# A block-DFT convolution with decimated rows, issued behind the FFN of the preceding chunk

## The chip, the cores and the metric

The program runs on one core of a Trainium2 chip. The metric is the device time in microseconds. Before the change the median of three runs is 472.5 us (472.4 to 473.94).

## The reference

Two layers, each made of a long convolution (H3 style) and a SwiGLU FFN, both added to the residual x. The sequence has 2048 rows of 512 channels, the FFN is 1792 wide. Inputs are bf16.

```python
k_shift = sum(k_pad[:, t:t + S, :] * shift_k[:, ks - 1 - t] for t in range(ks))   # ks = 4
kv = k_shift * v
y = irfft(rfft(pad(kv)) * rfft(pad(ssm_k)))[:S].astype(bf16) + kv * ssm_D          # along the sequence
A = lambda q: q * y
B = lambda x: (silu(x @ w_gate) * (x @ w_up)) @ w_down
x = A_q
for _ in range(2):
    x = x + A(layernorm(x))
    x = x + B(layernorm(x))
```

The convolution y depends on k, v, shift_k, ssm_k and ssm_D alone. It is the same in both layers and is needed row by row: the first 512 rows of x need the first 512 rows of y.

## The kernel before

The work has two stages, one after the other. **Convolution.** The sequence is cut into four blocks of 512 rows. For each block k and h (ssm_k) are loaded with a transposing DMA and v with a plain one (lines 115 to 129). `kv_block` multiplies 128-row pieces of k with 16 diagonal matrices of taps (256 matmuls of 128x128 in all, line 158) and VectorE multiplies by v (line 160). `forward` takes the odd-frequency DFT of a block, zero-padded to 1024 points, by 32 matmuls of 128x512 (line 171); ScalarE evacuates it to H or X (line 173). The tables are computed on the chip by `_gen_dft_table` (lines 23 to 49): VectorE makes the phase, ScalarE the sine and cosine. `product(i, j)` multiplies the spectra of block i of kv with block j of h and adds the result to Y of block i+j: six or eight VectorE operations of 128x2048 bf16 (lines 196 to 203), ten such pairs. `inverse(k)` turns Y of block k and, for the overlap, Y of block k-1 back into 512 rows: 64 matmuls of 128x512, 32 for block 0 (line 216).

**FFN.** Then, for each layer and each of four chunks of 512 rows: LayerNorm statistics (lines 288 to 298; the power runs on POOL), the convolution's residual in two f32 VectorE operations per 128 rows (lines 313, 315), statistics again, z on ScalarE (324), four transposes on TensorE (328), evacuation to zT (329), 14 steps of gate and up projections (335, 338) with sg on ScalarE (341) and hT_f on VectorE (342), and four down projections of 14 matmuls each (346), whose sum is added to x_sb in f32 (349) or stored (352, 353).

A scheduler orders the instructions of each engine by program order and its own costs. Pools set what may overlap: the weights (lines 231 to 245) take the place of the signal tiles, and the pools of the FFN that of the spectra, so no FFN instruction comes before the convolution's end.

Of the kernel before, what the change touches and what calls it, by code (L numbers as in the profile page):

```python
# [18 lines left out]
CONV_BLOCKS = 4  # L19
ROW_CHUNK = 512  # L20


def _gen_dft_table(nc, tabp, scr, L, kind, pidx):
    N = 2 * L
    KT = L // P
    FD = L if kind == "fwd" else N
    fr = scr.tile([P, FD], F32, name="fr")
    if kind == "fwd":
        nc.gpsimd.iota(fr[:], pattern=[[2, FD]], base=1, channel_multiplier=0, allow_small_or_imprecise_dtypes=True)
    else:  # L30
        nc.gpsimd.iota(fr[:], pattern=[[1, FD]], base=0, channel_multiplier=0, allow_small_or_imprecise_dtypes=True)
    cos_t = tabp.tile([P, KT, FD], BF16, name=f"{kind}_cos")
    nsin_t = tabp.tile([P, KT, FD], BF16, name=f"{kind}_nsin")
    for kt in range(KT):
        mult = scr.tile([P, 1], F32, name="mult")
        if kind == "fwd":
            nc.vector.tensor_scalar(out=mult[:], in0=pidx[:], scalar1=float(kt * P), scalar2=None, op0=ALU.add)
        else:
            nc.vector.tensor_scalar(out=mult[:], in0=pidx[:], scalar1=2.0, scalar2=float(2 * kt * P + 1),
                                    op0=ALU.mult, op1=ALU.add)  # L40
        prod = scr.tile([P, FD], I32, name="prod")
        nc.vector.tensor_scalar(out=prod[:], in0=fr[:], scalar1=mult[:], scalar2=float(N), op0=ALU.mult, op1=ALU.add)
        ms = scr.tile([P, FD], I32, name="ms")
        nc.vector.tensor_single_scalar(out=ms[:], in_=prod[:], scalar=2 * N - 1, op=ALU.bitwise_and)
        nc.scalar.activation(out=nsin_t[:, kt, :], in_=ms[:], func=ACT.Sin, scale=-math.pi / N, bias=math.pi)
        am = scr.tile([P, FD], F32, name="am")
        nc.scalar.activation(out=am[:], in_=ms[:], func=ACT.Abs, scale=1.0, bias=float(-N))
        nc.scalar.activation(out=cos_t[:, kt, :], in_=am[:], func=ACT.Sin, scale=-math.pi / N, bias=math.pi / 2)
    return cos_t, nsin_t
# [3 lines left out]
def kernel(  # L53
# [44 lines left out]
    ypool = tc.alloc_tile_pool(name="ypool", bufs=1, side="left")
    Y_sb = ypool.tile([P, NS, D], BF16, name="Y_sb")
    tabp = tc.alloc_tile_pool(name="tab", bufs=1, side="left")  # L100
    specp = tc.alloc_tile_pool(name="spec", bufs=1, side="left")
    ykp = tc.alloc_tile_pool(name="yk", bufs=4, side="left")
    tmpp = tc.alloc_tile_pool(name="ptmp", bufs=2, side="left")
    psc = tc.alloc_tile_pool(name="psc", bufs=2, space=PSUM)
    tscr = tc.alloc_tile_pool(name="tscr", bufs=1, side="right")
# [281 lines left out]
```

## Time and profile before

| what | value |
|---|---|
| median of three runs | 472.5 us (472.4 to 473.94) |
| span of the profiled execution | 472.5 us, 5517 instructions |
| TensorE matmul busy | 430.5 us, 91% |
| VectorE busy | 289.9 us, 61% |
| ScalarE busy | 167.1 us, 35% |
| chain that ended last | TensorE 70%, VectorE 15%, ScalarE 8% |

The profiled execution's own time is its span, 472.5 us, which is also the median. Busy shares are averages over the whole span. The convolution ends at 128.7 us, the first gate matmul starts at 146.8 us, and the last matmul ends at 468.6 us.

### The profile page before, as it was taken

What the parts mean: (1) busy time and instruction counts of PE and PEld (TensorE: products, weight loads), DVE (VectorE), ACT (ScalarE), POOL (GpSimd) and SP (SyncE); (2) the same over time, 40 slices, a digit from 0 to 9 for tenths busy, and PEclk for the clock granted to TensorE, in tenths of its full rate; (3) what the DMA queues carried; (4) which work ended last, traced back from release to release, by engine and by line L of the source; (5) the groups of instructions that cost most, each with busy time, mean ns of one, the idle gap of its engine ahead of it and who ended that gap; (6) DMA issues with size and microseconds to landing.
All of it is one profiled execution on the core that took longest, in us unless ns stands there. A gap on an engine that the chain in (4) does not pass through costs nothing.

```text
span 472.5 us, 5517 instructions
## 1 busy us (share of the span) xinstructions
PE 430.5 (91%) x2166; PEld 204.8 (43%) x2208; DVE 289.9 (61%) x473; ACT 167.1 (35%) x250; POOL 27.4 (6%) x43
## 2 busy tenths in 40 slices
PE   4999999999927997999999899999989999997996
PEld 3545545544403443444444444444434444443442
DVE  2649899999778899955763774684213423321431
ACT  4995444310115421631432353053153305303320
POOL 7000000000101201100000000000000000000000
PEclk9999999999976999899999999999989999998999
DMA  8925000670211000000000000000000000000001
GB/s 177 183 44 136 2 1 1 222 246 0 90 44 44 1 1 0 0 1 1 1 0 2 0 1 0 1 1 0 16 30 0 1 33 12 1 24 22 0 1 44
DMA packets 26779, 16.39 MB, mean 35 GB/s; under 512 B 17793, under 2 KB 25730, under 8 KB 26754
## 3 DMA queue, kind: packets, MB, share of 16 engines
q1 hardware_dynamic: 26754, 16.05, 12.4%
q8 instruction: 17, 0.28, 0.2%
q14 instruction: 8, 0.07, 0.0%
HBM read 9.70 MB, written 2.10 MB: 25 GB/s over the span
## 4 chain that ended last, share of the span: by engine, by line
PE 70%; DVE 15%; ACT 8%; issue 2%; POOL 1%; SPq 1%; DMA 1%; POOLq 0%; DVEq 0%; ACTq 0%
PE pd L346 19%; PE pu L338 18%; PE pg L335 18%; PE pi L216 10%; PE pf L171 5%; DVE bnst L292 3%; ACT zT L329 3%; DVE x_sb L315 2%; DVE hT_f L342 2%; ACT z L324 2%; POOL rstd L297 1%; DVE t L196 1%; DVE t L197 1%; ACT X L173 1%; ACT H L173 1%
## 5 line engine op out<-in xcount | busy, mean ns | idle before, releaser
L342 DVE TENSOR_TENSOR hT_f<-sg,pu 128x512 bf16<-128x512 bf16 x112 | 76.3, 684 | 90.2 <-PE pu L338 88.2
L335 PE MATMUL pg<-zT,wg_sb 128*128 128x512 bf16 x438 | 116.9, 387 | 4.2 <-ACT zT L329 3.4
L338 PE MATMUL pu<-zT,wu_sb 128*128 128x512 bf16 x439 | 116.8, 386 | 1.7 <-DVE hT_f L342 1.2
L341 ACT ACTIVATE sg<-pg 128x512 bf16<-128x512 f32 x112 | 66.8, 596 | 117.4 <-PE pg L335 110.6
L346 PE MATMUL pd<-wd_sb,hT_f 128*128 128x512 bf16 x438 | 97.8, 379 | 1.7 <-DVE x_sb L349 1.0
L335 PEld LDWEIGHTS <-wg_sb 128*128 128x128 bf16 x448 | 44.6, 99 | 57.8 <-issue 8.6
L338 PEld LDWEIGHTS <-wu_sb 128*128 128x128 bf16 x448 | 44.6, 100 | 56.9 <-issue 6.2
L346 PEld LDWEIGHTS <-hT_f 128*128 128x128 bf16 x448 | 43.8, 98 | 54.4 <-issue 1.3
L329 ACT COPY zT<-pt 128x512 bf16<-128x512 bf16 x32 | 17.8, 584 | 90.5 <-PE pt L328 90.4
L297 POOL TENSOR_TENSOR rstd<-ve,nhalf 128x4 f32<-128x4 f32 x16 | 18.0, 1128 | 288.7 <-DVE ve L295 261.2
L352 DVE TENSOR_TENSOR ot<-x_sb,pd 128x512 bf16<-128x512 f32 x16 | 11.0, 687 | 37.1 <-PE pd L346 37.1
L292 DVE BATCH_NORM_STATS2 bnst<-x_sb 128x6 f32<-128x512 f32 x48 | 31.7, 675 | 0.4
L328 PE MATMUL pt<-ident,z 128*128 128x128 bf16 x128 | 12.3, 232 | 20.6 <-ACT z L324 16.8
L324 ACT ACTIVATE z<-x_sb,nmr,rstd 128x512 bf16<-128x512 f32 x32 | 24.7, 807 | 8.9 <-DVE nmr L319 8.9
L158 PE MATMUL pk<-dg,kTb 128*128 128x128 bf16 x256 | 19.9, 232 | 8.6 <-DMA kTb<-in_A_k_dram 6.5
L216 PE MATMUL pi<-Yk,inv_nsin 128*128 128x512 bf16 x110 | 27.3, 379 | 0.2
L216 PE MATMUL pi<-Yk,inv_cos 128*128 128x512 bf16 x107 | 27.0, 379 | 0.1
L196 DVE TENSOR_TENSOR t<-X,H 128x2048 bf16<-128x2048 bf16 x20 | 24.3, 1215 | 3.4 <-ACT X L173 3.4
L173 ACT ACTIVATE X<-pf 128x1024 bf16<-128x1024 f32 x16 | 16.5, 1030 | 22.3 <-PE pf L171 22.2
L197 DVE TENSOR_TENSOR t<-X,H 128x2048 bf16<-128x2048 bf16 x20 | 24.3, 1215 | 0.0
L158 PEld LDWEIGHTS <-kTb 128*128 128x128 bf16 x256 | 17.4, 105 | 13.3 <-DMA kTb<-in_A_k_dram 6.5
L228 ACT CAST Y_sb<-pi 128x512 bf16<-128x512 f32 x16 | 9.4, 586 | 36.2 <-PE pi L216 30.7
(47 smaller groups left out, 312.4 us busy)
## 6 DMA issues: line engine op xcount, KB each, us to landing
vt<-in_A_v_dram SPq DMA_DIRECT2D x4, 512.0 KB, 4.3
xin<-in_A_q_dram SPq DMA_DIRECT2D x4, 512.0 KB, 3.6
out_dram<-ot SPq DMA_DIRECT2D x16, 128.0 KB, 1.7
wg_sb<-in_B_w_gate_dram SPq DMA_DIRECT2D x1, 1792.0 KB, 7.2
wu_sb<-in_B_w_up_dram SPq DMA_DIRECT2D x1, 1792.0 KB, 11.3
wd_sb<-in_B_w_down_dram SPq DMA_DIRECT2D x1, 1792.0 KB, 16.0
kTb<-in_A_k_dram SPq DMA_TRANSPOSE x4, 5.3
hTb<-in_A_ssm_k_dram SPq DMA_TRANSPOSE x4, 4.3
```

Of the source, the lines that this page charges most:

```text
L158: nc.tensor.matmul(ps[:, dt * P:(dt + 1) * P], lhsT=kTb[:, dt, c0 - j:c0 - j + P], rhs=dg[:, dt, j, :], start=(j == 0), stop=(j == KS - 1))
L196: nc.vector.tensor_mul(out=t1[:], in0=Xi[:, :, pa[0], :], in1=Hj[:, :, pa[1], :])
L197: nc.vector.tensor_mul(out=t2[:], in0=Xi[:, :, pb[0], :], in1=Hj[:, :, pb[1], :])
L216: nc.tensor.matmul(pss[m][:], lhsT=tab[:, ft, c0:c0 + P], rhs=Ysrc[:, ft, part, :], start=(cnt[m] == 0), stop=(cnt[m] == nmm - 1))
L292: nc.vector.bn_stats(out=st[:], in_=src_of_tile(i))
L324: nc.scalar.activation(out=z[:], in_=x_sb[:, n0 + i, :], func=ACT.Identity, scale=rstd[:, i:i + 1], bias=nmr[:, i:i + 1])
L329: nc.scalar.copy(out=zT[:, :, i * P:(i + 1) * P], in_=pt[:])
L335: nc.tensor.matmul(pg[:], lhsT=wg_sb[:, kd, ft * P:(ft + 1) * P], rhs=zT[:, kd, :], start=(kd == 0), stop=(kd == KD - 1))
L338: nc.tensor.matmul(pu[:], lhsT=wu_sb[:, kd, ft * P:(ft + 1) * P], rhs=zT[:, kd, :], start=(kd == 0), stop=(kd == KD - 1))
L341: nc.scalar.activation(out=sg[:], in_=pg[:], func=ACT.Silu)
L342: nc.vector.tensor_mul(out=hT_f[:, ft, :], in0=sg[:], in1=pu[:])
L346: nc.tensor.matmul(pd[:], lhsT=hT_f[:, ft, i * P:(i + 1) * P], rhs=wd_sb[:, ft, :], start=(ft == 0), stop=(ft == NF - 1))
```

## The change

The kernel is written anew in four respects; the FFN's own matmuls stay as they are.

*Rows decimated by four.* Rows r, r+4, r+8, ... of a block form one operand (partition p holds rows 4p to 4p+3), so a DFT of 512 rows becomes four short ones of 128, combined by butterflies. `half` does 16 matmuls of 128x512 per signal and block instead of 32, `butterfly` adds two VectorE operations. Two tables of 12 x 128 columns replace the larger ones (`table`). h is loaded without a transpose and turned by 16 TensorE transposes per block (`transpose_h`).

*Overlap folded into the kernel's spectra.* `spectrum_h(b)` combines the spectra of h of blocks b and b-1 into G[b] (two VectorE operations), so the product sum of a block holds its overlap, and `inverse` needs 16 matmuls per block instead of 64, after a `fold` of two VectorE operations.

*Order.* Only block 0 and the spectrum of h of block 1 come before the first FFN chunk, in an order that is written out by hand. `plan` lists what goes behind each FFN chunk, as generators; `tick` advances them after each of the 14 steps. The plan interleaves the layers: (layer 0, chunk 0), (0,1), (1,0), (0,2), (1,1), (0,3), (1,2), (1,3). After the hand-written part the scheduler orders the engines.

*Residual.* x is bf16. LayerNorm of the convolution's residual is n on ScalarE, then a multiply and an add on VectorE of 128x1024 bf16. The FFN's sum is added in place, and the result is stored from there.

```diff
+    def table(kind, src, mul):
+        ph = big.tile([P, NT, P], I32, name="ph", tag="s8")
+        for i, (_, r, quarter) in enumerate(BLOCKS):
+            nc.vector.tensor_scalar(out=ph[:, i, :], in0=src(r), scalar1=mul(r), scalar2=float(quarter * (N // 2)),
...
+        nc.vector.tensor_single_scalar(out=ph[:], in_=ph[:], scalar=2 * N - 1, op=ALU.bitwise_and)
+        tab = const.tile([P, NT, P], BF16, name=f"tab_{kind}")
+        nc.scalar.activation(out=tab[:], in_=ph[:], func=ACT.Sin, scale=-math.pi / N, bias=math.pi)
...
+    def half(rows, ev, dst, par, scale, ps_of, engines):
+        for key in ("ac", "bd")[par]:
+            slot = "abcd".index(key)
+            for part in (0, 1):
+                ps = ps_of()
+                mm(ps[:], [(fT(f, r), rows[:, r, :]) for f, r in FWD_TERMS[key][part]])
...
+    def butterfly(ev, dst, sl):
+        lo, hi = (slice(0, 2), slice(2, 4)) if sl is None else (sl, sl + 2)
+        nc.vector.tensor_tensor(out=dst[:, lo], in0=ev[:, lo], in1=ev[:, hi], op=ALU.add)
+        nc.vector.tensor_tensor(out=dst[:, hi], in0=ev[:, lo], in1=ev[:, hi], op=ALU.subtract)
...
+        nc.vector.tensor_tensor(out=G[b][:, :, 0, :], in0=H[b][:, :, 0, :], in1=Hp[:, :, 1, :], op=ALU.subtract)
...
+        nc.vector.tensor_tensor(out=G[b][:, :, 1, :], in0=H[b][:, :, 1, :], in1=Hp[:, :, 0, :], op=ALU.add)
...
+                   [(kTb[:, dt, PADL + r - j:PADL + r - j + R * (P - 1) + 1:R], dg[:, dt, j, :]) for j in range(KS)])
...
+        for pair in PAIRS:
+            for r in pair:
+                ps = ps_of()
+                mm(ps[:], terms[r])
+                nc.scalar.copy(out=Yk[:, r, :], in_=ps[:])
+                yield
...
+        for pair, n in zip(PAIRS, ns):
+            sl = slice(pair[0], pair[1] + 1, 2)
+            nc.vector.tensor_mul(out=n[:], in0=n[:], in1=Y[c][:, sl, :])
+            nc.vector.tensor_add(out=xc[:, sl, :], in0=xc[:, sl, :], in1=n[:])
...
+        def tick():
+            done[0] += 1
+            while done[1] * (8 if total < 20 else 13) < total * done[0]:
+                done[1] += 1
+                if next(g, g) is g:
+                    break
...
+        for ft in range(NF):
+            pg, pu = psf(), psf()
+            mm(pg[:], [(wts["g"][:, kd, ft * P:(ft + 1) * P], zT[:, kd]) for kd in range(KD)])
+            mm(pu[:], [(wts["u"][:, kd, ft * P:(ft + 1) * P], zT[:, kd]) for kd in range(KD)])
+            sg = work.tile([P, L], BF16, name="sg", bufs=2)
+            nc.scalar.activation(out=sg[:], in_=pg[:], func=ACT.Silu)
+            ht = work.tile([P, L], BF16, name="ht", bufs=14)
+            nc.vector.tensor_mul(out=ht[:], in0=sg[:], in1=pu[:])
+            hts.append(ht)
+            tick()
...
+    hgen = transpose_h(0, ("pf", 6))
+    drain(hgen)
+    stats0 = ln1_stats(0, 0)
+    together(shift_mul(0, psf), stats0)
...
+    load_weights("g")
+    load_h(1, nc.sync)
+    load_k(1)
+    load_v(1, nc.sync)
...
+    for par in (0, 1):
+        drain(half(hs, evh, G[0], par, 2.0 / N, psf, (nc.scalar, nc.scalar)),
+              half(vt, evx, X[0], par, 1.0, psf, (nc.scalar, nc.vector)))
+        butterfly(evh, G[0], par)
+        butterfly(evx, X[0], par)
+    f1 = spectrum_h(1)
+    for par in (0, 1):
+        for _ in product(0, 0, slice(par, 4, 2)):
+            if par == 0:
+                next(f1)
...
+    drain(inverse(0, psf, su), prol)
+    drain(f1)
...
+    plan = [
+        ((0, 0), [g_(x_only, 1), g_(spectrum_x, 1), g_(conv_products, 1), g_(inverse, 1),
+                  g_(prologue, 0, 1), g_(loads, 2), g_(eager, 1)]),
+        ((0, 1), [g_(prologue, 1, 0), g_(spectrum_h, 2), g_(spectrum_x, 2), g_(conv_products, 2)]),
+        ((1, 0), [g_(inverse, 2), g_(prologue, 0, 2), g_(loads, 3), g_(eager, 2), g_(spectrum_h, 3)]),
+        ((0, 2), [g_(prologue, 1, 1), g_(spectrum_x, 3), g_(conv_products, 3), g_(inverse, 3)]),
+        ((1, 1), [g_(prologue, 0, 3)]),
+        ((0, 3), [g_(prologue, 1, 2)]),
+        ((1, 2), [g_(prologue, 1, 3)]),
+        ((1, 3), []),
+    ]
+    BEHIND = {(0, 0): 55, (0, 1): 49, (1, 0): 45, (0, 2): 44, (1, 1): 10, (0, 3): 10, (1, 2): 10, (1, 3): 1}
```

PSUM's eight banks are divided: six (`pf`) for gate, up and down projections, two (`pc`) for the convolution and the transposes.

How the order of the instructions changes is shown at three places. First ScalarE, where before the first FFN chunk begins: the last evacuations of the inverse (Y_sb), z and zT, and then sg (the silu of a gate projection) without convolution work.

```order
L228 CAST Y_sb<-pi 128x512 x12
L324 ACTIVATE z<-x_sb,nmr,rstd 128x512 x3
L329 COPY zT<-pt 128x4x128 x2
L324 ACTIVATE z<-x_sb,nmr,rstd 128x512
L329 COPY zT<-pt 128x4x128 x2
L341 ACTIVATE sg<-pg 128x512 x4
```

The same place in the change: the first FFN chunk begins at the first sg, and behind it stand the evacuations ev of the forward DFT of block 1 and the normalised rows n of chunk 1.

```order
L363 COPY zT<-ptz 128x8x128
L415 ACTIVATE sg<-pf 128x512 x2
L183 ACTIVATE ev<-pc 128x512 x2
L331 ACTIVATE n<-xc,nmr,rstd 128x512
L183 ACTIVATE ev<-pc 128x512 x2
L415 ACTIVATE sg<-pf 128x512
L183 ACTIVATE ev<-pc 128x512 x2
L331 ACTIVATE n<-xc,nmr,rstd 128x512
L183 ACTIVATE ev<-pc 128x512 x2
L331 ACTIVATE n<-xc,nmr,rstd 128x512
L415 ACTIVATE sg<-pf 128x512
```

Eight evacuations and three n now stand between the second and the fourth sg.

Second VectorE at the end of FFN chunk (0,0) of the change. su is the folded spectrum of block 1, t and Z are products for block 2, n and xc the residual of chunk 1, ht the product of silu and up projection.

```order
L268 TENSOR_TENSOR su<-Z 128x2048
L269 TENSOR_TENSOR su<-Z 128x2048
L250 TENSOR_TENSOR t_925<-X_626,G_520 128x2048
L252 TENSOR_TENSOR t_926<-X_626,G_520 128x2048
L368 TENSOR_TENSOR n<-n,Yk 128x1024
L256 TENSOR_TENSOR Z<-t_925,t_926 128x4x512
L369 TENSOR_TENSOR xc<-xc,n 128x2x512
L368 TENSOR_TENSOR n<-n,Yk 128x1024
L317 BN_STATS bnst<-xc 128x6
L369 TENSOR_TENSOR xc<-xc,n 128x2x512
L318 BN_AGGR mv<-bnst 128x2
L417 TENSOR_TENSOR ht<-sg,pf 128x512
```

The last row is the twelfth of the chunk's 14 ht; before, all products stood ahead of the first hT_f.

Third the SP queue's loads at the start of the change.

```order
L89 DMA_TRANSPOSE kTb<-in_A_k_dram 128x4x512
L101 DMA xc<-in_A_q_dram 128x2048
L113 DMA wg_sb<-in_B_w_gate_dram 128x4x1792
L113 DMA wu_sb<-in_B_w_up_dram 128x4x1792
L113 DMA wd_sb<-in_B_w_down_dram 128x14x512
L82 DMA hn<-in_A_ssm_k_dram 128x4x512
L91 DMA_TRANSPOSE kTb<-in_A_k_dram 128x4x528
```

The weights, which were issued after all loads of the convolution, now stand ahead of the h and k of block 1.

## Rows read from the trace of the kernel before

**Rows 1.** Page, part 1: busy us (share of the span) and instructions of each engine.
```profile
PE 430.5 (91%) x2166; PEld 204.8 (43%) x2208; DVE 289.9 (61%) x473; ACT 167.1 (35%) x250; POOL 27.4 (6%) x43
```
**Rows 2.** Windows by stage: length, busy us of each engine, granted clock, DMA share, GB/s.
```profile
40.00:128.70 88.70, 86.60 (x497) 43.47 (x506) 85.89 (x88) 28.69 (x34) 1.40 (x1) 1.00 0.29 92
128.70:146.80 18.10, 6.48 (x35) 3.25 (x35) 12.64 (x30) 6.12 (x10) 2.45 (x2) 0.71 0.09 29
146.80:307.90 161.10, 152.84 (x712) 69.67 (x727) 113.05 (x228) 51.31 (x85) 12.19 (x11) 0.98 0.01 4
307.90:468.60 160.70, 152.41 (x719) 70.00 (x729) 56.41 (x90) 49.88 (x83) 2.01 (x2) 0.98 0.04 13
468.60:472.50 3.90, 0.00 (x0) 0.00 (x0) 0.69 (x1) 0.00 (x0) 0.00 (x0) 0.79 0.10 34
```
**Rows 3.** Timeline of TensorE in the last FFN chunk: start, duration, instructions.
```profile
426.98 0.61 PE L328 MATMUL pt<-ident,z 128*128 128x128 bf16 x8
...
433.87 1.03 PE L335 MATMUL pg<-zT,wg_sb 128*128 128x512 bf16 x4
434.74 1.03 PE L338 MATMUL pu<-zT,wu_sb 128*128 128x512 bf16 x4
```
**Rows 4.** The chain that ended last, at the shift matmuls: start, share of the chain.
```profile
40.04 1.05 PE pk L158 x16
```
**Rows 5.** Timeline of VectorE, in the products and in the first FFN chunk.
```profile
96.22 1.22 DVE L197 TENSOR_TENSOR t<-X,H 128x2048 bf16<-128x2048 bf16 x1
97.36 1.21 DVE L196 TENSOR_TENSOR t<-X,H 128x2048 bf16<-128x2048 bf16 x1
...
152.20 0.67 DVE L342 TENSOR_TENSOR hT_f<-sg,pu 128x512 bf16<-128x512 bf16 x1
152.79 0.24 DVE L293 BATCH_NORM_AGGREGATE mv<-bnst 128x2 f32<-128x6 f32 x2
```
**Rows 6.** Groups of VectorE by line and shape: count, busy us, mean ns, idle before.
```profile
L349 DVE TENSOR_TENSOR x_sb<-x_sb,pd 128x512 f32<-128x512 f32 x16 | 10.9, 684 | 12.2 <-PE pd L346 12.2
L160 DVE TENSOR_TENSOR kvb<-pk,vt 128x512 bf16<-128x512 f32 x16 | 10.6, 680 | 6.0 <-DMA vt<-in_A_v_dram 6.0
L42 DVE TENSOR_SCALAR prod<-fr,mult 128x1024 int32<-128x1024 f32 x4 | 3.0, 748 | 0.1
L44 DVE TENSOR_SCALAR ms<-prod 128x1024 int32<-128x1024 int32 x4 | 2.8, 695 | 8.1 <-ACT am L47 8.0
L42 DVE TENSOR_SCALAR prod<-fr,mult 128x512 int32<-128x512 f32 x4 | 2.0, 488 | 0.7 <-POOL fr L29 0.6
```
**Rows 7.** Groups of ScalarE and POOL, the same view.
```profile
L341 ACT ACTIVATE sg<-pg 128x512 bf16<-128x512 f32 x112 | 66.8, 596 | 117.4 <-PE pg L335 110.6 <-PE pu L338 5.6 <-DVE ve L295 1.1
L324 ACT ACTIVATE z<-x_sb,nmr,rstd 128x512 bf16<-128x512 f32 x32 | 24.7, 807 | 8.9 <-DVE nmr L319 8.9
L297 POOL TENSOR_TENSOR rstd<-ve,nhalf 128x4 f32<-128x4 f32 x16 | 18.0, 1128 | 288.7 <-DVE ve L295 261.2 <-ACT zT L329 27.5
L173 ACT ACTIVATE X<-pf 128x1024 bf16<-128x1024 f32 x16 | 16.5, 1030 | 22.3 <-PE pf L171 22.2
L96 ACT ACT_TABLE_LOAD x1 | 1.3, 1283 | 0.7 <-PEq L371 0.7
```
**Rows 8.** Page, part 6, DMA issues: count, KB, us from issue to landing.
```profile
wg_sb<-in_B_w_gate_dram SPq DMA_DIRECT2D x1, 1792.0 KB, 7.2
wu_sb<-in_B_w_up_dram SPq DMA_DIRECT2D x1, 1792.0 KB, 11.3
wd_sb<-in_B_w_down_dram SPq DMA_DIRECT2D x1, 1792.0 KB, 16.0
```
**Rows 9.** Timeline of TensorE at the first gate and up matmuls.
```profile
146.77 1.87 PE L335 MATMUL pg<-zT,wg_sb 128*128 128x512 bf16 x4 [0.67 <-ACT zT L329]
...
148.44 1.79 PE L338 MATMUL pu<-zT,wu_sb 128*128 128x512 bf16 x4
```
**Rows 10.** Group of TensorE's weight loads at the shift matmuls.
```profile
L158 PEld LDWEIGHTS <-kTb 128*128 128x128 bf16 x256 | 17.4, 105 | 13.3 <-DMA kTb<-in_A_k_dram 6.5 <-issue 4.2
```

More of the change, by code (lines that the diff above doesn't have):

```diff
@@ L17 @@
 LN_EPS = 1e-5
[L19 to L49, printed above, removed]
+NB = 4
+R = 4
+BLOCKS = [("C", 0, 1), ("C", 1, 1), ("C", 2, 1), ("C", 3, 1),
+          ("nS", 0, 2), ("nS", 1, 2), ("nS", 2, 2), ("nS", 3, 2),
+          ("nC", 1, 3), ("nC", 2, 3), ("S", 2, 0), ("S", 3, 0)]
+BI = {(f, r): i for i, (f, r, _) in enumerate(BLOCKS)}
 @with_exitstack
@@ L98 @@
[L98 to L105, printed above, removed]
@@ new lines, in drain, with together, ffn, run @@
+    def drain(*gens):
+        for g in gens:
+            for _ in g:
+                pass
+    def together(*gens):
+        gens = list(gens)
+        while gens:
+            for g in list(gens):
+                if next(g, gens) is gens:
+                    gens.remove(g)
+    def ffn(layer, c, behind):
+        steps = NF + R
+        def run():
+            for g in behind:
+                yield from g()
+        g = run()
+        total = BEHIND[layer, c]
+        done = [0, 0]
+        def tick():
[4 more added lines that the diff above has]
+                    break
+        xc, zT = xs[c], zts.pop((layer, c))
+        hts = []
+        for ft in range(NF):
[8 more added lines that the diff above has]
+            tick()
+        for i in range(R):
+            pd = psf()
+            mm(pd[:], [(hts[ft][:, i * P:(i + 1) * P], wts["d"][:, ft, :]) for ft in range(NF)])
+            nc.vector.tensor_add(out=xc[:, i, :], in0=xc[:, i, :], in1=pd[:])
+            if layer == 1:
+                nc.sync.dma_start(out=o_t[:, c, i, :], in_=xc[:, i, :])
+            tick()
+        drain(g)
@@ new lines, with loads @@
+    f1 = spectrum_h(1)
+    for par in (0, 1):
+        for _ in product(0, 0, slice(par, 4, 2)):
+            if par == 0:
+                next(f1)
+        if par == 0:
+            prol = prologue(0, 0, True)
+            next(prol)
+        fold(Z[0], su, par)
+    Z.pop(0)
+    drain(inverse(0, psf, su), prol)
+    drain(f1)
+    manual.__exit__(None, None, None)
+    def loads(b):
+        load_h(b, nc.sync)
+        load_k(b)
+        load_v(b, nc.sync)
+        load_x(b)
+        yield
@@ L356 @@
+    BEHIND = {(0, 0): 55, (0, 1): 49, (1, 0): 45, (0, 2): 44, (1, 1): 10, (0, 3): 10, (1, 2): 10, (1, 3): 1}
+    for (layer, c), behind in plan:
+        ffn(layer, c, behind)
+    for pool in (psp, work, small, xp, wp, big, ldp, const):
         pool.release()
```

477 lines of the change are left out of this document (249 added, 228 removed), and 4 rows, old and new, of the table FWD_TERMS.

## The prediction

> **What bounds the kernel now.** I read the page first, then windows by stage, then groups by line, then timelines. TensorE is busy for 91% of the span [rows 1], but an average over stages hides the structure, so the windows come next [rows 2]. From 40 to 128.7 us both TensorE (86.6 of 88.7) and VectorE (85.9) are full: the convolution is bound by both. From 128.7 to 146.8 neither is: TensorE has 6.5 us of work while the first LayerNorms run as a chain, and its clock falls to 0.71. After that TensorE is alone at 95%, VectorE is at 70% in the first half of the FFN stage and 35% in the second. So there is free VectorE and ScalarE time where TensorE is full, and the question is whether convolution work can be put there.
>
> Prices. A 128x512 matmul in a stream costs 0.216 us (four start 0.87 apart), a transpose about 0.08 (eight in 0.61) [rows 3], a 128x128 shift matmul 0.065 (16 in 1.05) [rows 4]. On VectorE a 128x2048 bf16 operation takes 1.135 start to start, a 128x512 operation with a PSUM operand 0.60 [rows 5]. Nothing shows a 128x1024 bf16 one; it lies between half of 1.135 and the 0.60, and I take 0.60.
>
> **The sum on TensorE.** Removed: 256 forward and 224 inverse matmuls become 128 and 64, 288 fewer, 62 us. Added: 64 transposes of h, 5 us. Of the transposes the Trainium skill says more (TensorE: Matmul & The Clock Gate, Part 4: PE-mode transpose): about 275 ns each in a kernel, with the full clock not engaging. By that page the 64 would cost 18 us rather than 5; the trace has eight in 0.61 us, so the row decides.
> FFN chunks, named (layer, chunk), have 168 matmuls, 36.3 us each. With what is issued behind them TensorE needs: (0,0) shift 4.2, forward of x 3.5, inverse 3.5, 16 transposes 1.3: 48.8. (0,1) transposes 1.3, h transposes 1.3, two forwards 7.0, shift 4.2: 50.1. (1,0) inverse 3.5, transposes 2.6, one forward 3.5: 45.9. (0,2) transposes 1.3, shift 4.2, forward 3.5: 45.3. (1,1) inverse 3.5 and transposes: 41.1. Then 37.6, 37.6, 36.3. Sum 342.7.
>
> **The start**, which nothing covers. VectorE builds both tables: 24 operations of 128 columns, between a quarter of the 0.49 at 512, 0.12, and all of it; 0.488 at 512 and 0.748 at 1024 lie on a line that gives 0.29, less some overlap 0.25; and two ANDs over 1536 at 0.85 (0.695 at 1024) [rows 6]: 7.7 us from about 1.2. Four diagonal tables 2.4, four shift products and four bn_stats 5.3, then a wait for the POOL power and nmr 1.5: 18.5. Then 4 evacuations, 8 butterflies, 12 product operations, 4 folds, 28 x 0.6: 35. TensorE and ScalarE run beside it: the 12 evacuations of ScalarE at 0.6 and a second table load of 1.28 end before VectorE needs them. Then a chain, by [rows 7]: two inverse groups and copies 1.5, multiply, add, statistics 2.7, POOL 1.1, the same again for the second pair with two foreign bn_stats 5, two z at 0.8, transposes, the 1024-wide copy 1.0: 49. Block 1 of h is issued behind the three weights, which landed 7, 11 and 16 us after their issue [rows 8], so with those issued near 5 it lands near 24, where TensorE has done block 0's forwards by about 22; VectorE's 35 covers that, 6 us more would show. Through this stretch TensorE works in pieces; after an idle of that kind eight matmuls took 0.43 each [rows 9], so I add 2: the FFN starts at **51**.
>
> **Stalls behind the chunks.** VectorE needs in the first four chunks 48.8, 46.6, 41.9 and 44.3 us (each 18 operations of 0.6 for ht and the residual, a prologue of 8.4, in three of them four shift products, and 24, 22, 20 and 20 operations of 2048), no more than TensorE, but its order is fixed, and the last ht of a chunk, without which no down projection closes, stands behind convolution work.
> (0,0): the eight evacuations of X1 go through two banks, mixed with sg and n on ScalarE, and end at chunk time 15; VectorE has had one ht since 9. From 15 to the last ht stand 22 2048-wide operations (25), 11 ht (6.6), the prologue (5.8) and waits for Yk and POOL (1.7): 54. What is left of the down projections and the z, zT tail end at 56.5, plus 1.7 for a half clock after the wait: 9.5 over TensorE's sum.
> (0,1): ScalarE has from 14 to 31.5 four z, two zT, two hs, eight evacuations, five sg and two n, where TensorE alone would be there at 27: 5.
> (1,0): from the last ht of (0,1), 11 before the boundary, VectorE has 35 2048-wide operations (39.7), 18 of 0.6 and a prologue: last ht at 45.3, then ten matmuls: 2 over.
> (0,2): last ht at 37, then 45 matmuls: 3.5 over. Later chunks: 0.5. Sum 20.5.
>
> **Edits that I cost at nothing.** The bf16 residual: an add from PSUM took 0.684 with an f32 partner and a shift product 0.680 with a bf16 one [rows 6], so no gain; the f32 pair of LayerNorm operations becomes ScalarE n plus two 1024-wide ones, inside the counts above. Each block's three loads are issued a chunk ahead on SP; the last x waits there for four outputs of (1,0), which leave 28 us before (0,2) reads it; if that cover went it would cost the 3 to 4 us of a load. Weight loads with a column step of 4, 320 of them: no row shows one. Loads at an odd column offset run inside the 0.065 of a shift matmul; at worst each would take its own 0.105 [rows 10], so 0 to 13 us, and I take 0, the nearest row; a gain is excluded since the columns stay 128. The new table load, 1.3, lies beside the diagonal tables.
>
> **Total**: 51 + 342.7 + 20.5 + 3.9 for the last add and store, as in the last window of [rows 2]: **418 us**, against a profiled execution whose span of 472.5 is the median of the runs, too.
>
> **Rivals.**
> Full overlap: the banks and the order let TensorE run through, as it did at 98% from 40 to 128.7 beside a full VectorE [rows 2]. Against it: the order above. Time 51 + 342.7 + 1.5 + 3.9 = 399. Chance 0.12.
> No cover for the down projections: each of the first four chunks costs VectorE's sum and then the 12.1 us of 56 matmuls, 182 + 48 = 230; with 51, (1,1) 41.5, 111.5 and 3.9 this is 438. For it: ht stands last in VectorE's order; against it: pieces of all four down projections are issued before it. Chance 0.13.
> Slower, the clock: waits inside the four chunks keep TensorE at 1.2 GHz, as after the idle before 146.8 [rows 9]. The Trainium skill bears on it (TensorE: Matmul & The Clock Gate, Why this matters for your kernels): it asks to avoid idle gaps between bursts of matmuls, which send the clock to half. In the trace the second half of the FFN, with a gap at each boundary, still had 0.98 [rows 2]. At half clock throughout, the four chunks' 190 us would be 380 and the kernel 588. It is slower than now if they take over 265 in all (472.5 less 51, 41.5, 111.5 and 3.9), that is with 40% of their matmul time at the lower level. Chance 0.03.
> The change doesn't do what it says: the interleaving collapses and each chunk waits for its convolution. The 103 us of VectorE work of the convolution stand between chunks of 40.2, as before: 51 + 103 + 322 + 4 = 480. The order on TensorE speaks against it. Chance 0.02.
>
> **How the numbers follow.** My forecast has 0.70: 418, on its own 403 to 435 (6 us of start either way, half of the stalls gone, or the 13 of the weight loads). 0.12 lies at 399 and 0.13 at 438, so the range is 399 to 445. A measurement of this kernel can tell 0.3%, 1.4 us, from no change. Faster: 0.70 + 0.12 + 0.13 = 0.95. The 0.05 of the last two is slower with 0.04, and 0.01 for a milder form of them that ends at the present time.
>
> **What would show it.** Right: the first gate matmul near 49 to 51; (0,0) the longest chunk, near 58, with VectorE idle from 9 to 15 in it and TensorE waiting for VectorE before the down projections close; the last three chunks 36 to 38 each, back to back, without the pause of the boundaries now; granted clock above 0.9 from there. Shift matmuls at 0.065. Wrong: a first gate matmul past 57, shift matmuls above 0.1, a granted clock under 0.75 in the first four chunks, or boundaries that still pause for z.

## The result and the profile after

The changed kernel takes 417.57 us (median of four runs, 417.13 to 418.2), the kernel before 473.22 on the same chip: ratio 0.8815 (95% interval 0.8783 to 0.8846). The forecast was 418. The profiled execution took 417.13 us, 1.8 of it outside its span of 415.3. In every execution on record 1.7 to 2.1 us lie outside the span, the kernel before included (472.39 against 470.6), so that its span of 472.5 equals its median of 472.5 by chance only: the profiled execution before took some 474 us. Executions that a slow state lengthened are left out of the medians below.

Page, part 1 (columns as in [rows 1]):

```profile
PE 370.3 (89%) x1947; PEld 178.3 (43%) x1984; DVE 301.3 (73%) x504; ACT 178.7 (43%) x281; POOL 19.9 (5%) x27
```

Windows by stage, cut at the first gate matmul of each chunk (columns as in [rows 2]): the start, (0,0), (0,1), (1,0), (0,2), (1,1), (0,3), (1,2), (1,3), the tail.

```profile
0.00:52.86 52.86, 29.02 (x186) 17.49 (x189) 44.67 (x100) 30.35 (x43) 4.16 (x13) 0.86 0.64 204
52.86:107.94 55.08, 49.22 (x263) 23.23 (x268) 48.88 (x66) 21.93 (x36) 2.01 (x2) 0.98 0.08 20
107.94:160.27 52.33, 49.54 (x291) 24.67 (x296) 41.05 (x70) 28.50 (x47) 3.02 (x3) 1.00 0.12 31
160.27:208.67 48.40, 45.96 (x229) 21.01 (x232) 47.37 (x61) 20.74 (x34) 1.82 (x1) 1.00 0.00 1
208.67:256.88 48.21, 45.45 (x261) 22.21 (x265) 43.18 (x73) 22.51 (x36) 3.83 (x3) 1.00 0.07 22
256.88:299.05 42.17, 40.73 (x198) 18.81 (x201) 29.23 (x60) 19.21 (x30) 3.02 (x3) 1.00 0.03 10
299.05:336.20 37.15, 36.94 (x182) 17.33 (x185) 15.02 (x24) 11.70 (x18) 0.00 (x0) 1.00 0.01 5
336.20:375.40 39.20, 37.19 (x181) 17.17 (x184) 18.78 (x36) 15.35 (x24) 2.01 (x2) 1.00 0.03 11
375.40:411.80 36.40, 36.24 (x166) 16.34 (x167) 12.39 (x18) 8.36 (x14) 0.00 (x0) 1.00 0.04 15
411.80:415.30 3.50, 0.04 (x1) 0.00 (x0) 0.69 (x1) 0.00 (x0) 0.00 (x0) 1.00 0.11 37
```

TensorE has lost 60 us of work (430.5 to 370.3) and VectorE has gained 11, yet the stage from 40 to 128.7 us in which both were full [rows 2] is gone: what is left of it lies in the windows two to five, where TensorE is at 89 to 95% beside a VectorE at 78 to 98%. The pauses at the chunks' boundaries, which left the FFN at 95%, are gone too, but for the one after (0,0), where TensorE waits 2.2 us for z and zT.

### The profile page after: what moved, and what is told of

Same layout as the page of the kernel before. It is cut to its first block, busy times and chain, and to the rows that moved or that the text cites. A ratio compares the mean times of both kernels' runs of the same rounds, so it can differ in the third digit from the quotient of the medians.

```text
span 415.3 us, 5086 instructions
## 1 busy us (share of the span) xinstructions
PE 370.3 (89%) x1947; PEld 178.3 (43%) x1984; DVE 301.3 (73%) x504; ACT 178.7 (43%) x281; POOL 19.9 (5%) x27
## 4 chain that ended last, share of the span: by engine, by line
PE 46%; DVE 34%; ACT 8%; issue 5%; DMA 4%; POOL 2%; POOLq 0%; DVEq 0%; ACTq 0%
PE pf L158 38%; PE pc L158 5%; DVE bnst L317 4%; DVE ht L417 4%; DMA hn<-in_A_ssm_k_dram 4%; DVE t L252 3%; DVE t L259 3%; DVE t L250 3%; DVE Z L261 3%; ACT z L331 2%; POOL rstd L323 2%; ACT ev L183 2%; DVE n L368 2%; DVE xc L369 2%; DVE xc L423 1%
## 5 line engine op out<-in xcount | busy, mean ns | idle before, releaser
L415 ACT ACTIVATE sg<-pf 128x512 bf16<-128x512 f32 x112 | 66.4, 597 | 160.9 <-PE pf L158 125.3
L158 PE MATMUL pf<-zT,wg_sb 128*128 128x512 bf16 x435 | 115.9, 380 | 5.7 <-DVE ht L417 4.0
L158 PE MATMUL pf<-zT,wu_sb 128*128 128x512 bf16 x436 | 115.8, 380 | 0.7
L417 DVE TENSOR_TENSOR ht<-sg,pf 128x512 bf16<-128x512 bf16 x112 | 76.5, 684 | 52.7 <-PE pf L158 44.2
L158 PE MATMUL pf<-wd_sb,ht 128*128 128x512 bf16 x438 | 99.8, 379 | 1.5 <-DVE ht L417 0.9
L158 PEld LDWEIGHTS <-ht 128*128 128x128 bf16 x448 | 43.5, 98 | 53.7 <-DVE ht L417 2.4
L423 DVE TENSOR_TENSOR xc<-xc,pf 128x512 bf16<-128x512 bf16 x32 | 21.5, 687 | 32.5 <-PE pf L158 32.5
L317 DVE BATCH_NORM_STATS2 bnst<-xc 128x6 f32<-128x512 bf16 x64 | 42.3, 682 | 0.3
L323 POOL TENSOR_TENSOR rstd<-ve,nhalf 128x4 f32<-128x4 f32 (+1 forms) x17 | 18.1, 1067 | 330.4 <-DVE ve L321 317.7
L183 ACT ACTIVATE ev<-pc 128x512 bf16<-128x512 f32 x48 | 27.0, 611 | 12.0 <-PE pc L158 11.9
L331 ACT ACTIVATE n<-xc,nmr,rstd 128x512 bf16<-128x512 bf16 x32 | 24.9, 821 | 4.7 <-DVE nmr L325 4.7
L250 DVE TENSOR_TENSOR t<-X,G 128x2048 bf16<-128x2048 bf16 (+1 forms) x22 | 24.8, 1127 | 0.1
L252 DVE TENSOR_TENSOR t<-X,G 128x2048 bf16<-128x2048 bf16 (+1 forms) x22 | 24.8, 1126 | 0.0
```

The costliest lines, as they stand in the source:

```text
L158: nc.tensor.matmul(o, lhsT=lhsT, rhs=rhs, start=(n == 0), stop=(n == len(terms) - 1))
L183: nc.scalar.activation(out=ev[:, slot, part], in_=ps[:], func=ACT.Copy, scale=scale)
L250: nc.vector.tensor_mul(out=t1[:], in0=Xi[:, sl, 0, :], in1=Gj[:, sl, part, :])
L252: nc.vector.tensor_mul(out=t2[:], in0=Xi[:, sl, 1, :], in1=Gj[:, sl, 1 - part, :])
L317: nc.vector.bn_stats(out=st[:], in_=xc[:, i, :])
L323: nc.gpsimd.tensor_tensor(out=rstd[:], in0=ve[:], in1=nhalf[:].to_broadcast((P, n)), op=ALU.pow)
```

## Experiments

Each run is timed beside the kernel before on the same chip; ratios are to that.

**1. The order alone.** The pieces come after a chunk's last down projection instead of between its matmuls.

```diff
-    BEHIND = {(0, 0): 55, (0, 1): 49, (1, 0): 45, (0, 2): 44, (1, 1): 10, (0, 3): 10, (1, 2): 10, (1, 3): 1}
+    BEHIND = dict.fromkeys([(l, c) for l in (0, 1) for c in range(NB)], 0)
```

> All pieces of the convolution are issued behind the last down projection of a chunk instead of between its matmuls; nothing else is changed. Theory (the interleaved order gives a large part of the gain): the convolution of block 1 then stands bare between chunks (0,0) and (0,1), some 40 us of VectorE work (14 products of 1.135, folds, evacuations, a prologue), and parts of blocks 2 and 3 stand bare too: 450 to 480 us. Rival (the gain is the 288 fewer matmuls alone, and the engines find the overlap without being told): 418 to 430 us.

Measured: 491.64 us, ratio 1.0385 (1.0349 to 1.0421), slower than the kernel before and above both expectations. Between the chunks (0,0) and (0,1), windows (the second is this gap) and the timeline of TensorE (start, duration, instruction, idle before and who ended it):

```profile
52.67:89.80 37.13, 36.75 (x166) 16.69 (x170) 15.86 (x24) 10.94 (x18) 1.01 (x1) 0.98 0.00 1
89.80:140.28 50.48, 15.36 (x101) 7.87 (x101) 38.49 (x53) 13.21 (x21) 2.02 (x2) 0.69 0.09 21
```
```profile
118.26 5.74 PE L158 MATMUL pc<-su,tab_inv 128*128 128x512 bf16 x16 [19.85 <-DVE su L268]
133.85 1.31 PE L361 MATMUL ptz<-ident,z 128*128 128x128 bf16 x8 [9.85 <-ACT z L331]
```

The gap of 50 us is block 1's products, inverse and LayerNorm, bare on VectorE, and TensorE's granted clock in it is 0.69. The saving of matmuls without the interleaving loses 17 us; the interleaving is worth 74. What it hides in this gap is VectorE's work (38.5 us) more than TensorE's (15.4).

**2. TensorE's sum.** Each group of DFT matmuls behind the chunks is issued twice.

```diff
-                mm(ps[:], [(fT(f, r), rows[:, r, :]) for f, r in FWD_TERMS[key][part]])
+                for _ in range(times[0]):
+                    mm(ps[:], [(fT(f, r), rows[:, r, :]) for f, r in FWD_TERMS[key][part]])
...
-                mm(ps[:], terms[r])
+                for _ in range(times[0]):
+                    mm(ps[:], terms[r])
...
     manual.__exit__(None, None, None)
+    times[0] = 2
```

> Behind the chunks each group of forward and inverse DFT matmuls is issued twice into the same bank, the second overwriting the first: 128 more matmuls of 128x512, 27.6 us of TensorE, spread as 32 over each of the first four chunks or nearly so; VectorE and ScalarE have the same work as before. Theory (TensorE's sum sets the chunks, so a removed DFT matmul is worth its 0.216 us less what the waits inside a chunk absorb): between 27.6 less the 14 us of waits seen in the first four chunks and 27.6, so 431 to 445 us, likeliest 438. Rival (the order on VectorE and ScalarE sets these chunks, and fewer DFT matmuls brought little): 418 to 424 us.

Measured: 442.25 us (441.95 to 442.44), ratio 0.9339 (0.9303 to 0.9376). The windows of the first four chunks:

```profile
52.73:114.57 61.84, 56.76 (x295) 26.65 (x301) 50.40 (x72) 22.36 (x36) 2.01 (x2) 0.97 0.07 18
114.57:173.94 59.37, 56.65 (x322) 27.74 (x329) 45.36 (x69) 28.67 (x46) 3.02 (x3) 1.00 0.10 27
173.94:229.38 55.44, 52.58 (x260) 24.11 (x264) 52.57 (x80) 24.16 (x38) 2.01 (x2) 1.00 0.02 6
229.38:286.70 57.32, 55.20 (x307) 26.94 (x312) 42.87 (x67) 22.67 (x36) 3.53 (x3) 1.00 0.04 14
```

24.7 of the 27.6 us appear in the time: a matmul added to these chunks costs nine tenths of its 0.216 us, and the waits inside them take up hardly any of it. That one taken out gains as much is likely by this, but no run took any out. (The last window also has the inverse of block 3, which lay in (1,1); that chunk fell to 37.2.)

**3 to 6. The start.** In the changed kernel VectorE waits 2.73 us for Yk between its last fold and the first residual operation:

```profile
36.60 0.69 DVE L269 TENSOR_TENSOR su<-Z 128x1024 bf16<-128x1024 bf16 x1
40.01 0.69 DVE L368 TENSOR_TENSOR n<-n,Yk 128x1024 bf16<-128x1024 bf16 x1 [2.73 <-ACT Yk L290]
```

Three things stand ahead of Yk: the load of h of block 1, which took 16.46 us from its issue (chain of waits) and stopped TensorE for 4.1; four n on ScalarE; and the fold of the odd half. The fold has to be there. `inverse` makes rows 0 and 2 first, out of s and u, then rows 1 and 3 out of t and w (slots 0 to 3 of su are s, u, t, w); the fold of the even half writes s and t, that of the odd half u and w, so even the first row needs both. Experiment 3 loads h early, into a buffer of its own.

```diff
-        hn = ldp.tile([P, KD, L], BF16, name="hn")
+        hn = big.tile([P, KD, L], BF16, name="hn", tag="s8") if b == 1 else ldp.tile([P, KD, L], BF16, name="hn")
...
     load_x(0)
+    load_h(1, nc.sync)
...
     load_weights("g")
-    load_h(1, nc.sync)
```

> The load of h of block 1 goes to a buffer of its own and is issued ahead of the three weights instead of behind them. Theory A (it is on the path: TensorE waits 4.1 us for it, the eight evacuations and the four n follow it on ScalarE, and the first product with Yk waits 2.7 us behind them): that wait goes, the first gate matmul comes at about 50.2 instead of 52.9, and the time falls by 2.0 to 2.7 us to about 415. Theory B, as the prediction had it (VectorE's own work covers the late load): no change, 417 to 418. Rival C (the early load takes bandwidth from k, v and x of block 0, which are wanted first): 1 to 3 us slower.

Measured: 417.43 us, ratio 0.8819 (0.8796 to 0.8842): no change, as the prediction had it. TensorE, then a window of its inverse, then VectorE (the fold of the odd half, addition and subtraction, then the residual):

```profile
31.11 0.59 PE L159 MATMUL pf<-su,tab_inv 128*128 128x512 bf16 x2 [2.05 <-DVE su L269]
36.42 4.47 PE L159 MATMUL pf<-su,tab_inv 128*128 128x512 bf16 x14 [4.72 <-DVE su L269]
```
```profile
36.42:40.90 4.48, 4.47 (x14) 1.57 (x13) 1.62 (x3) 1.76 (x3) 0.00 (x0) 0.71 0.00 0
```
```profile
35.67 0.69 DVE L269 TENSOR_TENSOR su<-Z 128x1024 bf16<-128x1024 bf16 x1
36.28 0.69 DVE L270 TENSOR_TENSOR su<-Z 128x1024 bf16<-128x1024 bf16 x1
...
39.79 0.69 DVE L369 TENSOR_TENSOR n<-n,Yk 128x1024 bf16<-128x1024 bf16 x1 [2.82 <-ACT Yk L291]
```

With the load gone TensorE waits 4.72 us for the fold of the odd half, and after that idle its fourteen matmuls run at a granted clock of 0.71 (4.47 us against 3.18 before). They start 0.06 us after the addition that makes u has ended, while the subtraction into the same buffer still runs: they wait for their operand and not for the whole buffer. Yk is as late as it was: the cover is VectorE's work ahead of the fold, and then the clock. The four n are done at 32.5 here, 5 us before ScalarE's first Yk, so they stand in the way only while the load is late. Experiment 4 moves n ahead instead.

```diff
+    prol = prologue(0, 0, True)
+    next(prol)
     for par in (0, 1):
         for _ in product(0, 0, slice(par, 4, 2)):
```

> The four normalised rows n of chunk (0,0) are issued on ScalarE ahead of the evacuations of block 1's h instead of behind them; the load stays late. Theory (the 2.7 us wait for Yk is partly ScalarE's order): the n run while ScalarE waits for the load, Yk follows the inverse matmuls directly, which themselves still stand behind the h forward on TensorE: the wait shrinks from 2.7 to about 1.4 us, the first gate matmul comes at about 51.5, and the time falls by 1 to 1.5 us to about 416.3. Rival (the wait is the late load alone): no change.

Measured: 416.17 us (416.03 to 416.55), ratio 0.8788 (0.8768 to 0.8808); the wait is 1.56 us and the first gate matmul at 51.69, as the theory had it. Two groups of inverse matmuls and a copy are what is left in it. Experiment 5 adds a buffer for each half of su.

```diff
-        s, u, t, w = (su[:, i] for i in range(4))
+        s, u, t, w = (su[i % 2][:, i // 2] for i in (0, 2, 1, 3)) if type(su) is list else (su[:, i] for i in range(4))
...
-    su = big.tile([P, 4, 2, D], BF16, name="su", tag="s8")
+    su = [big.tile([P, 2, 2, D], BF16, name=f"su{i}", tag="s8") for i in range(2)]
```

> As the run with n issued early, and the folded spectrum su of block 0 lies in two buffers, one for the even and one for the odd half. In the run with the early load TensorE stood idle for 4.7 us in front of the inverse until VectorE had folded the odd half, though its next eight matmuls read the even half alone. Theory (that wait comes from the two halves being one buffer): the first eight inverse matmuls run right behind the h forward, Yk is there when VectorE has folded, the wait for Yk (2.7 us in the changed kernel, 1.56 with n early) falls under 0.6, and the time is 415 to 415.4. Rival (the matmuls wait for the fold for another reason): as with n early alone, 416.2.

Measured: 416.38 us, ratio 0.879 (0.8765 to 0.8815), as without it. TensorE:

```profile
27.19 1.90 PE L208 MATMUL pt<-ident,hn 128*128 128x128 bf16 x16 [5.52 <-DMA hn<-in_A_ssm_k_dram]
...
36.27 3.62 PE L158 MATMUL pf<-su,tab_inv 128*128 128x512 bf16 x16
```

The sixteen matmuls run in one piece, but they start at 36.27 as before, since the late load now holds everything ahead of them. The edit also does more than its expectation says. Its list hands over the slots 0, 2, 1, 3 as s, u, t, w, so u and t change places: the first eight matmuls read the even half alone because they get t for u, and the rows of block 0 come out as another sum than the convolution. In the changed kernel the third matmul already reads u, so the theory that one buffer causes the wait is refuted by experiment 3, and experiments 5, 6, 9 and 10, which contain this list, time a kernel that leaves a dependency out. Experiment 6 has all three edits.

> The three edits of the start together: h of block 1 loaded ahead of the weights, n issued early, su in two buffers. Each of the first two and the pair of the last two left one of three things standing ahead of the first product with Yk: the late load, the order on ScalarE, or the fold of the odd half. Theory (three covers of the same wait: it goes only when all are taken away): the first eight inverse matmuls run by 34, VectorE goes on at about 37 without a wait, the first gate matmul comes near 50.3 instead of 52.9, 414.5 to 415.2 us. Rival (what is then bare is a half clock on TensorE, or VectorE itself): 416 to 417.

Measured: 414.32 us (414.28 to 414.38), ratio 0.8746 (0.872 to 0.8771), 3.25 us under the changed kernel. VectorE, then TensorE:

```profile
35.68 0.69 DVE L270 TENSOR_TENSOR su<-Z 128x1024 bf16<-128x1024 bf16 x1
36.29 0.68 DVE L271 TENSOR_TENSOR su<-Z 128x1024 bf16<-128x1024 bf16 x1
36.89 0.68 DVE L370 TENSOR_TENSOR n<-n,Yk 128x1024 bf16<-128x1024 bf16 x1
```
```profile
32.21 1.89 PE L159 MATMUL pf<-su,tab_inv 128*128 128x512 bf16 x8
36.42 3.57 PE L159 MATMUL pf<-su,tab_inv 128*128 128x512 bf16 x8 [2.33 <-DVE su L270]
...
49.73 0.59 PE L159 MATMUL pf<-zT,wg_sb 128*128 128x512 bf16 x1
```

The wait is gone and the FFN starts 3.13 us earlier, which is the gain. But the first eight matmuls run at 32.21, some 4 us before u is there (35.68 + 0.69), which the convolution does not allow, so 414.32 is not a time of this kernel. Of the runs that keep the dependency the early n gained 1.4 us and the early load nothing; the two together were not run.

**7. X1's evacuations, shared.** In (0,0) VectorE idles before its fourth ht and X1's butterfly follows:

```profile
66.18 0.69 DVE L417 TENSOR_TENSOR ht<-sg,pf 128x512 bf16<-128x512 bf16 x1 [4.25 <-PE pf L158]
66.92 1.23 DVE L188 TENSOR_TENSOR X<-ev 128x2048 bf16<-128x2048 bf16 x1
```
```diff
-    yield from forward(sig.pop((b, "v")), X[b], 1.0)
+    yield from forward(sig.pop((b, "v")), X[b], 1.0, (nc.scalar, nc.vector) if b == 1 else (nc.scalar, nc.scalar))
```

> Of the eight evacuations of X1 in chunk (0,0) four go to VectorE, which is idle for 4.25 us there; the rest stays. Theory (the eight evacuations through ScalarE start VectorE's products late, and the last ht of the chunk and TensorE's 5.9 us of waits follow from that): the butterfly of X1 starts about 2 us earlier (66.9 to 65), the waits of TensorE in (0,0) shrink from 5.9 to about 4, and the time falls by 1.5 to 2 us, to 415.5 to 416. Rival (the waits come from the total of VectorE's work behind that point, and the added 2.4 us on VectorE eat the gain): 417 to 418, or 0.5 slower.

Measured: 418.09 us (416.94 to 419.09), ratio 0.8821 (0.8794 to 0.8847): no gain. VectorE there:

```profile
63.34 0.69 DVE L181 TENSOR_SCALAR ev<-pc 128x512 bf16<-128x512 f32 x1 [0.68 <-PE pc L158]
65.20 0.69 DVE L181 TENSOR_SCALAR ev<-pc 128x512 bf16<-128x512 f32 x1 [1.17 <-PE pc L158]
...
67.67 1.23 DVE L188 TENSOR_TENSOR X<-ev 128x2048 bf16<-128x2048 bf16 x1
```

Each evacuation on VectorE waits for TensorE, whose forward matmuls stand between gate and up projections, and the butterfly starts no sooner (67.67; the FFN had started 0.54 later). So ScalarE's evacuations alone did not make it late; TensorE's order and the two banks of `pc` remain, and no run separates these two.

**8. Products of block 2 moved on**, from (0,0) to (0,1).

```diff
-                  g_(prologue, 0, 1), g_(loads, 2), g_(eager, 1)]),
-        ((0, 1), [g_(prologue, 1, 0), g_(spectrum_h, 2), g_(spectrum_x, 2), g_(conv_products, 2)]),
+                  g_(prologue, 0, 1), g_(loads, 2)]),
+        ((0, 1), [g_(prologue, 1, 0), g_(eager, 1), g_(spectrum_h, 2), g_(spectrum_x, 2), g_(conv_products, 2)]),
...
-    BEHIND = {(0, 0): 55, (0, 1): 49, (1, 0): 45, (0, 2): 44, (1, 1): 10, (0, 3): 10, (1, 2): 10, (1, 3): 1}
+    BEHIND = {(0, 0): 49, (0, 1): 55, (1, 0): 45, (0, 2): 44, (1, 1): 10, (0, 3): 10, (1, 2): 10, (1, 3): 1}
```

> The six product operations of block 2 that stood at the end of chunk (0,0) (6.8 us of VectorE) move behind chunk (0,1). Theory (a chunk waits for its last ht, which stands behind convolution work on VectorE): VectorE's 48.9 us in (0,0) fall to 42, its waits on TensorE from 5.9 to 3 us; (0,1), with 41 us of VectorE work in 52, has room for them: the time falls by 2 to 3 us, to 414.5 to 415.5. Rival (the same work is only late one chunk further on: (0,1) is bound by its own convolution, which now starts 6.8 us later): (0,0) gains as much as (0,1) to (0,2) lose, 417 to 420.

Measured: 419.52 us (418.63 to 420.32), ratio 0.885 (0.8826 to 0.8874): 2 us slower, and (0,0) itself is longer (56.3 us from gate matmul to gate matmul, against 55.1). First TensorE in the changed kernel at the end of (0,0), then in this one, then VectorE in this one:

```profile
97.09 5.79 PE L158 MATMUL pf<-wd_sb,ht 128*128 128x512 bf16 x26 [0.93 <-DVE ht L417]
103.64 0.40 PE L361 MATMUL ptz<-ident,z 128*128 128x128 bf16 x4 [0.76 <-ACT z L331]
...
108.16 1.02 PE L158 MATMUL pf<-zT,wg_sb 128*128 128x512 bf16 x3 [1.10 <-ACT zT L363]
```
```profile
104.31 0.40 PE L361 MATMUL ptz<-ident,z 128*128 128x128 bf16 x4 [0.85 <-ACT z L331]
...
107.33 0.61 PE L361 MATMUL ptz<-ident,z 128*128 128x128 bf16 x4 [1.22 <-ACT z L331]
109.04 0.58 PE L158 MATMUL pf<-zT,wg_sb 128*128 128x512 bf16 x1 [1.10 <-ACT zT L363]
```
```profile
92.77 1.21 DVE L250 TENSOR_TENSOR t<-X,G 128x2048 bf16<-128x2048 bf16 x1
93.90 0.68 DVE L368 TENSOR_TENSOR n<-n,Yk 128x1024 bf16<-128x1024 bf16 x1
94.50 1.21 DVE L252 TENSOR_TENSOR t<-X,G 128x2048 bf16<-128x2048 bf16 x1
```

The wait for the last ht before the down projections is gone; the wait for z of the next chunk, which hangs on block 1's convolution and its LayerNorm, has taken its place. The time is the rival's, its mechanism is not: (0,0) gains nothing, since with less work ahead of the last ht (at 92.2 instead of 103.8) another thing holds its end. Part of that is the edit itself. The moved products hardly leave the chunk: VectorE is busy for 49.4 us in it, not 42, and two of them stand at 92.77 and 94.50 among the residual of chunk 1. And `BEHIND` spreads the 49 pieces that stay over as many steps as the 55 before, so that residual begins at 93.90 instead of 92.13. No run separates these from the theory's cause.

**9 and 10. The rate of the pieces**, on top of experiment 6, with which alone they are compared: all out after 10 of a chunk's 18 steps (14 of gate and up projections, four of down projections) instead of 13, or after 16.

```diff
-            while done[1] * (8 if total < 20 else 13) < total * done[0]:
+            while done[1] * (8 if total < 20 else 10) < total * done[0]:
```

> On top of the three edits of the start: in the first four chunks the pieces of the convolution are issued at a rate that has them all out after 10 of the 18 steps of a chunk instead of 13. Theory X (the end of such a chunk is set by the chain of the next block: products, inverse, LayerNorm, zT, which VectorE now reaches sooner): TensorE's waits in the first four chunks, some 14 us, shrink by 1 to 3 us against the run with the three edits. Theory Y, as the prediction had it (it is set by the last ht, which now stands behind more of the convolution): 1 to 4 us longer than that run.

> As the run before, with all pieces out after 16 of the 18 steps. Theory X (the chain of the next block sets the end of a chunk): 2 to 6 us longer than the run with the three edits, and the added time is a wait for z or zT at the boundaries. Theory Y (the last ht sets it): 1 to 3 us shorter, since the ht come sooner.

Measured at 10: 419.64 us (418.89 to 420.37), 5.3 more than experiment 6; at 16: 417.49, with single runs from 414.37 to 417.64. TensorE at the end of (0,0), at 10 and then at 16:

```profile
99.80 3.64 PE L159 MATMUL pf<-wd_sb,ht 128*128 128x512 bf16 x10 [3.56 <-DVE ht L419]
```
```profile
103.99 0.40 PE L363 MATMUL ptz<-ident,z 128*128 128x128 bf16 x4 [1.41 <-ACT z L333]
...
107.01 0.40 PE L363 MATMUL ptz<-ident,z 128*128 128x128 bf16 x4 [1.21 <-ACT z L333]
```

Issued faster, TensorE waits for the last ht (theory Y); slower, for z (theory X). 13 lies between. How much 16 costs stays open: in its profiled run eight gate and up matmuls that followed a wait of 2.12 us ran at a granted clock of 0.56, as did some at 10, and two of its six runs were as fast as experiment 6.

**11 and 12. The bf16 residual alone**, in the kernel before.

```diff
-    x_sb = xpool.tile([P, NS, D], F32, name="x_sb")
+    x_sb = xpool.tile([P, NS, D], BF16, name="x_sb")
...
-                t = work.tile([P, D], F32, name="t")
+                t = work.tile([P, D], BF16, name="t")
```

> One part of the change alone, put into the kernel before: its residual x and the product t ahead of it are bf16 instead of f32. Theory, as the prediction had it (the element type of the residual is worth nothing by itself: an add from a bank takes 0.684 us with an f32 partner and 0.687 with a bf16 one): the time of the kernel before within 0.3%, ratio 0.997 to 1.003. Rival (VectorE handles the bf16 scalar_tensor_tensor operations in half of their 0.745 us, and eight of them stand in each boundary between chunks): 3 us for the first boundary and 1 to 1.5 for each later one that TensorE waits for, 462 to 468 us, ratio 0.98 to 0.99.

Measured: 483.82 us, ratio 1.0225 (1.0182 to 1.0268), which neither theory had. Groups of VectorE, then its timeline at the first LayerNorm:

```profile
L313 DVE SCALAR_TENSOR_TENSOR t<-x_sb,mv,Y_sb 128x512 bf16<-128x512 bf16 x16 | 11.9, 746 | 0.3
...
L349 DVE TENSOR_TENSOR x_sb<-x_sb,pd 128x512 bf16<-128x512 bf16 x16 | 10.9, 684 | 12.2 <-PE pd L346 12.2
```
```profile
137.03 1.29 DVE L292 BATCH_NORM_STATS2 bnst<-xin 128x6 f32<-128x512 bf16 x2 [13.79 <-DMA xin<-in_A_q_dram]
```

The operations take what they took in f32 (the add 684 ns, as in [rows 6]; the product with Y 746, and 746 before); the load of x was issued at 133.49 instead of 119.09, behind the last inverse matmuls. In the kernel before the first chunk's statistics start at 124.43, while the last inverse matmuls run until 132.8, so its two stages do overlap by some 8 us, and the late load took this away. The smaller tiles had moved the others in memory. Experiment 12 has the same types, in tiles of the old size.

```diff
+    x_sb = xpool.tile([P, NS, 2, D], BF16, name="x_sb")[:, :, 0, :]
...
+                t = work.tile([P, 2, D], BF16, name="t")[:, 0, :]
```

> As the run with the bf16 residual in the kernel before, but x and t keep the bytes that they had as f32 (every second row of 512 is left unused), so that every other buffer lies where it lay. In the earlier run each operation took what it took in f32 (0.745 against 0.746), and yet the first LayerNorm waited 13.8 us for x, whose load was issued 14 us later. Theory (the 10 us came from another place in memory, whose release the load of x waits for, and the element type is worth nothing): the time of the kernel before, ratio 0.997 to 1.003. Rival (the type itself costs time somewhere): ratio 1.01 to 1.025 again.

Measured: 473.16 us, ratio 0.9987 (0.9966 to 1.0008). The type is worth nothing here; the 10 us were the load's place.

## Why the prediction was right, point by point

- **TensorE's sum, 342.7.** Measured in the eight windows: 341.3. By chunk 49.2, 49.5, 46.0, 45.5, 40.7, 36.9, 37.2, 36.2. Experiment 2 shows that work added to this sum appears in the time. The 64 transposes of h, half of them in the start, take 5.4 busy in all, as the prediction had it. Its 18 was an estimate from the 275 ns of the Trainium skill (TensorE: Matmul & The Clock Gate, Part 4: PE-mode transpose): one is recorded with 243 ns here, near that figure, but they overlap, and eight take 0.61 us. The page also has the full clock not engage for them; the trace disagrees, since in (0,1) the granted clock was 1.00.
- **The start, 51.** Measured 52.9. VectorE came to its last fold at 37.3 rather than 35: its 28 operations of 0.60 took 17.9 us, since eight that need the one before to be done start 0.12 later, and the shift products waited 1.5 for TensorE. (The terms up to 18.5 add up to 18.1.) From that fold to the first gate matmul it took 15.6, against 14 and the 2 added for TensorE in pieces; 1.2 of the 1.6 above 14 is the late Yk (2.73 against 1.5). h of block 1 landed at 26.7, not 24, and "VectorE's 35 covers that" does not hold: the late load put the four n in front of Yk, and moving them ahead brought 1.4 us (experiment 4). Loaded early it gained nothing: TensorE then stood idle for 4.72 us, its clock fell, and its fourteen matmuls took 1.3 us longer (experiment 3). The 1024-wide operation is 0.60 start to start, as taken.
- **Stalls, 20.5.** Measured 17.7 (sum of the windows less their TensorE work): 5.9, 2.8, 2.4 and 2.8 against 9.5, 5, 2 and 3.5, later 3.8 against 0.5. In (0,0) the step was over-sized and its reason half right: the last ht came at chunk time 50.9, not 54, and experiments 8 and 10 have z of the next chunk as a limit right behind it. Experiment 7 speaks against ScalarE's evacuations alone as the cause of VectorE's idle there. In (1,0) and (0,2) the last ht came at 45.5 and 38.1, near the 45.3 and 37 of the prediction, but TensorE shows no wait for it. Of the 13.9 us in the first four chunks some 5 are waits for an ht, most of them in mid-chunk (2.12 at the longest, in (0,0)), and some 6 for z or zT: at the end of (0,0), as predicted, in (0,1), where the prediction had ScalarE's queue (ScalarE itself waited 0.80 for nmr ahead of that z), and in (1,0), where it had none:

```profile
84.28 1.02 PE L158 MATMUL pf<-zT,wg_sb 128*128 128x512 bf16 x3 [2.12 <-DVE ht L417]
...
124.65 0.40 PE L361 MATMUL ptz<-ident,z 128*128 128x128 bf16 x4 [1.87 <-ACT z L331]
...
186.50 0.40 PE L361 MATMUL ptz<-ident,z 128*128 128x128 bf16 x4 [1.20 <-ACT z L331]
```

So the size of this term is right within 3 us, its cause in part only. The 1.7 for a half clock after the wait did not show in this run. Of the 3.8 in later chunks 2.0 lie in (1,2), where TensorE waits 1.80 for z, which I had not counted, and 1.4 in (1,1).

- **Edits at nothing.** The residual's type is worth nothing, as taken (experiment 12, in the kernel before). The weight loads with a column step are free behind the chunks, where the shift matmuls run at 0.061 (32 in 1.95), though such a load takes 114 ns there instead of 105 [rows 10]. They are not in the start: there 64 shift matmuls took 5.74 us (0.09 each) with loads of 138 ns, and VectorE waited 1.5 us for them. The kernel before has slow shift matmuls at its start too (16 in 1.91 at 10.76), and no run changed the column step alone, so what makes them slow is open.
- **Rivals.** The collapse, with its chance of 0.02, was priced at 480; in experiment 1, which brings it about, it is 492: (0,0) to (0,1) and (1,0) to (0,2) each stand bare, and TensorE's matmuls are busy for 386.8 us instead of 370.3, at a granted clock of 0.69 to 0.98. Full overlap and no cover lie 19 and 20 us from what was measured. The clock stayed at 0.98 or more in the mean of every chunk here; where TensorE was left idle (experiments 1, 3, 6, 9, 10) it was 0.52 to 0.71 in the gap or right behind. The Trainium skill (TensorE: Matmul & The Clock Gate, Why this matters for your kernels) asks to avoid idle gaps between bursts of matmuls, since the clock goes back to half behind them; experiment 3 agrees. Of the prediction's signs of being wrong one appeared, a boundary that pauses for z, after (0,0).
- **Luck.** The misses of +1.9 at the start, -1.4 of TensorE, -2.8 of stalls, -0.4 at the tail and +1.8 outside the span, which the sum left out, cancel to within a microsecond. That the stalls of (0,1) to (0,2) came near in size while part of their waits were others is luck too.
